# One store of the gradient of wo in two parts: 115 rows and 13 rows

## The chip, the cores and the metric

The kernel runs on one core of one Trainium2 chip. The metric is the device time of one execution in microseconds (us); of several runs the median is taken. The core has five engines with a queue of instructions each (PE for matmuls, DVE, ACT, POOL, and SP, which here only issues transfers) and 16 DMA engines, which carry all transfers between HBM and on-chip memory. SP's transfers are on queue q1 of the profile, ACT's on q10, POOL's on q0.

## The reference

The program is the forward and backward pass of a small decoder block: attention with one query token per sequence over a cache of keys and values, and a ReLU layer behind it, both with layer norm and residual.

```python
B, Sq, D = 2, 1, 640
Hq, Hkv, Sk, Dh = 32, 32, 4096, 128          # wo is (Hq * Dh, D) = (4096, 640)
q = (x @ wq).reshape(B, Sq, Hq, Dh)
p = softmax(einsum("bhqd,bhkd->bhqk", q, k) * Dh ** -0.5)
o = einsum("bhqk,bhkd->bhqd", p, v)
attn = o.reshape(B, Sq, Hq * Dh) @ wo
h  = x + attn(layernorm(x))
h2 = h + relu(layernorm(h) @ w1) @ w2
# returned: h2 and the gradients of x, k_cache, v_cache, wq, wo, w1, w2 for grad_out
```

The gradient of wo (`out_5`, 4096 x 640 in bf16) is the outer product of `o` and the gradient of `h`, summed over the two sequences. The gradients of the two caches are 64 MB each and make up nearly all that is written.

## The kernel before

The work runs in two passes over the 64 pairs of sequence and head, each pair having a key tile and a value tile of 1 MB (128 rows of 8192 B). The first pass reads both, transposes the keys on PE, forms scores and softmax, and sums the values. The second pass reads most value tiles once more, and forms one gradient tile for the values (`gV`, stored by POOL at L911) and one for the keys (`gK`, stored by POOL at L862), both made by DVE at L843. Loads are issued by SP in the order of a list written at build time (K and V tiles and the tiles of the second pass at L463, the second reading of wq at L1025).

All large tiles share a set of buffers of 1 MB. A buffer has a kind that a planner moves as the kernel goes on: "ld" for loads, "g" for `gV` and `gK`, "f" for the tiles of the weight gradients (`ot`), "q" for tiles of wq. A buffer is taken again when all of its transfer has landed, so DVE's next write into a "g" buffer waits until the last of the 16 DMA engines has finished the store from it.

The weight gradients are a background task, `fin_gen`, which is advanced by small credits between the steps of the second pass; all is settled at build time. It calls `outer_rows` for each piece of an output. For the gradient of wo there are two calls, one for each half of the 4096 rows (`s0` is 0 and 16 in heads; 2048 rows each). In a call, row `p * 16 + c` of the half belongs to partition `p` (0 to 127) and place `c` (0 to 15). The 16 places are done in groups of 6, 6 and 4, beginning at `c0` = 0, 6 and 12. For each group the function takes an "f" buffer, makes the products by matmuls of at most 512 columns (L972), copies them to bf16 on ACT (L978), and issues one store for the group on ACT's queue (L981). With six places a partition's part is 6 x 640 x 2 = 7680 contiguous bytes in HBM, so this store is 128 rows of 7680 B, 960 KB.

The six groups of this gradient are the six stores of 7680 B and 5120 B rows that are issued from 684 us to 761 us, three for each half. The store that the change touches is the second of the first half, issued at 698.21 us. Three "f" buffers go round: the next tile in the buffer of this store has its first copy at 740.76 us.

Beside it there are rows of 256 B that `store_row` (L664) puts out through SP: four stores of five rows each, for the two short outputs, two at about 798 us and two at 864.08 and 867.42 us.

Of the kernel before, what the change touches and what calls it, by code (L numbers as in the profile page):

```python
# [15 lines left out]
def kernel(  # L16
# [20 lines left out]
    nc = tc.nc  # L37

    B, Sq, D = A_x.shape
# [34 lines left out]
    def pst(shape, dtype, role, name):  # L74

        k = banks[role].pop(0)
        banks[role].append(k)
        return ps.tile(shape, dtype, tag=f"bank{k}", bufs=1, name=name)
# [11 lines left out]
    def take(tag, shape, name):  # L90
        assert free[tag] > 0, (tag, name)
        free[tag] -= 1
        k = homes[tag].pop(0)
        t = pools[k].tile(shape, BF16, tag=f"big{k}", bufs=1, name=name)
        home_of[id(t)] = (tag, k, t)
        return t
# [9 lines left out]
    def give(t, to=None, first=False):  # L106
        tag, k, _ = home_of.pop(id(t))
        to = to or goes_to(tag)
        owned[tag] -= 1
        owned[to] += 1  # L110
        free[to] += 1
        homes[to].insert(0 if first else len(homes[to]), k)
        given_at[k] = step[0]
# [8 lines left out]
    def rested(tag, n):  # L122

        return free[tag] > 0 and (forced[0] or step[0] >= given_at.get(homes[tag][0], -n) + n)
# [24 lines left out]
    def wait(n):  # L149

        end = step[0] + n * spread[0]
        while step[0] < end and not forced[0]:
            yield 0.0
        yield
# [763 lines left out]
    def rows_of(pool, col, n, name, tag):  # L918

        r = pool.tile([128, n * 128], BF16, tag=tag, bufs=2 if tag == "rD" else 1, name=name)  # L920

        def widen(c0):
            cn = min(4, n - c0)
            w = FIN["wide"][(c0 // 4) % 2]
            nc.scalar.copy(out=w[:, 0:cn, :, 0:B], in_=col[:, c0:c0 + cn, None, :].to_broadcast([128, cn, 4, B]))

        widen(0)
        yield
        yield
        for c0 in range(0, n, 4):  # L930
            cn = min(4, n - c0)
            w = FIN["wide"][(c0 // 4) % 2]
            o_busy.append(banks["o"][0])
            t = pst([128, 512], FP32, "o", "rw_ps")
            for k in range(cn):
                nc.tensor.matmul(t[:, k * 128:(k + 1) * 128], lhsT=w[:, k, :, :].rearrange("p q x -> p (q x)"),  # L936
                                 rhs=ident_bf[:], start=True, stop=True)
            nc.scalar.copy(out=r[:, c0 * 128:(c0 + cn) * 128], in_=t[:, 0:cn * 128])
            o_busy.pop(0)
            if c0 + 4 < n:  # L940
                widen(c0 + 4)
                yield 1.0
            yield 0.7
        FIN[name] = r

    FIN = {}
# [2 lines left out]
    spreading = [False]  # L949
    o_busy = []  # L950

    def outer_rows(L, r0, nrow, R, N, out_ap, cc):


        P = nrow // cc
        grp = max(1, min(cc, 4096 // N))
        out_v = out_ap.rearrange("(p c) n -> p c n", c=cc)
        for c0 in range(0, cc, grp):
            gn = min(grp, cc - c0)
            while not rested("f", 13):  # L960
                yield 0.0
            ot = take("f", [128, grp, N], "ot")
            todo = [(k, n0, min(512, N - n0)) for k in range(gn) for n0 in range(0, N, 512)]
            made = []
            for x in range(len(todo) + 1):
                if x < len(todo):
                    k, n0, nn = todo[x]
                    q = 32 * (fw[0] % 4)
                    o_busy.append(banks["o"][0])
                    o_ps = pst([128, 512], FP32, "o", "o_ps")  # L970
                    fw[0] += 1
                    nc.tensor.matmul(o_ps[0:P, 0:nn], lhsT=L[q:q + B, bass.ds(r0 + c0 + k, P, step=cc)],  # L972
                                     rhs=R[q:q + B, n0:n0 + nn], start=True, stop=True)
                    made.append((o_ps, k, n0, nn))
                    yield 0.3
                if x > 0:
                    o_ps, k, n0, nn = made[x - 1]
                    nc.scalar.copy(out=ot[0:P, k, n0:n0 + nn], in_=o_ps[0:P, 0:nn])  # L978
                    o_busy.pop(0)
                    yield 0.3  # L980
            nc.scalar.dma_start(out=out_v[:, c0:c0 + gn, :], in_=ot[0:P, 0:gn, :])  # L981
            give(ot)

    def fin_gen(fin):
        FIN["wide"] = [fin.tile([128, 4, 4, 32], BF16, tag="wide", bufs=2, name="wide") for _ in range(2)]
        for w in FIN["wide"]:
            nc.vector.memset(w[:], 0.0)
        yield from wait(2)
        yield from rows_of(fin, acol, NF, "ar", "rX")
        ar_ps = pst([128, NFF, B], FP32, "mid", "ar_ps")  # L990
        for cf in range(NFF):
            nc.tensor.matmul(ar_ps[:, cf, :], lhsT=FIN["ar"][0:B, bass.ds(cf, 128, step=NFF)], rhs=ident_bf[0:B, 0:B],
                             start=True, stop=True)
        nc.scalar.copy(out=arow[:, 0:NFF, :], in_=ar_ps[:])
        if F_rem:
            nc.scalar.copy(out=arow[:, NFF, :], in_=acol[:, NFF, :])
        yield ("arow", 0)
        yield from rows_of(fin, gc, ND, "gr", "rD")
        yield from outer_rows(FIN["ar"], 0, NFF * 128, FIN["gr"], D, out_7[0:NFF * 128, :], NFF)
        if F_rem:  # L1000
            yield from outer_rows(FIN["ar"], NFF * 128, F_rem, FIN["gr"], D, out_7[NFF * 128:Dff, :], 1)
        yield from rows_of(fin, ghfc, NF, "ghfr", "rX")
        yield from rows_of(fin, x2c, ND, "x2r", "rD")
        yield from outer_rows(FIN["x2r"], 0, D, FIN["ghfr"], Dff, out_6, ND)
        HH = H // 2
        while ("gh1", B - 1) not in done:
            yield
        yield from rows_of(fin, gh1c, ND, "gh1r", "rD")
        for s0 in range(0, H, HH):
            yield from rows_of(fin, OFc[:, s0:s0 + HH, :], HH, "OFr", "rX")  # L1010
            yield from outer_rows(FIN["OFr"], 0, HH * 128, FIN["gh1r"], D, out_5[s0 * 128:(s0 + HH) * 128, :], HH)
        yield from rows_of(fin, x1c, ND, "x1r", "rD")
        for s0 in range(0, H, HH):
            while not all(("go", B - 1, h) in done for h in range(s0, s0 + HH)):
                yield
            yield from rows_of(fin, GQc[:, s0:s0 + HH, :], HH, "GQr", "rX")
            yield from outer_rows(FIN["x1r"], 0, D, FIN["GQr"], HH * 128, out_4[:, s0 * 128:(s0 + HH) * 128], ND)
# [165 lines left out]
    for n, (i, j) in enumerate(plan):  # L1183
# [29 lines left out]
        if i is None and ("w1", 1) in done and fin is None:  # L1213
            wts.release()
            fin = tc.alloc_tile_pool(name="fin", bufs=1)
            big2 = tc.alloc_tile_pool(name="big2", bufs=1)
            more_home("f", big2)
            banks.update(sps=[2, 3], o=[4, 5, 6])
            bg2.append(("fin", fin_gen(fin)))
            bg3.append(("gx", gx_gen(fin)))  # L1220
# [23 lines left out]
        at = LIGHT if j is None else HEAVY_TAIL if open_tail else HEAVY  # L1244
# [63 lines left out]
```

## Time and profile before

| What | Value |
|---|---|
| Median of 3 runs | 892.14 us (891.62 to 892.43) |
| Profiled execution, its own time | 892.4 us |
| Its span, first to last instruction | 890.6 us |
| Busy: PE, DVE, ACT, POOL | 83%, 77%, 53%, 23% of the span |
| DMA packets, bytes, mean rate | 56304, 361.84 MB, 406 GB/s |
| Share of the DMA queues q1 (SP), q0 (POOL), q10 (ACT) | 58.1%, 36.2%, 4.1% of 16 engines |
| Last gradient tile: issue of its store | 874.91 us |

The page of the profile has the busy share of each engine over the whole span and in 40 equal slices (a digit is tenths; 9 is 90% or more), the rate of the DMA engines in the same slices, the DMA queues, the chain of work that ended last, and the costliest groups of instructions. A DMA is cut into packets, here one for each contiguous run of at most 8192 B for these tiles, and a 4 B packet closes the share of each DMA engine that takes part; the transfer is complete when all of them have closed. The trace keeps of every packet its queue, size, start and duration, but not which of the 16 engines moved it.

### The profile page before, as it was taken

What the parts mean: (1) busy time and instruction counts of PE and PEld (TensorE: products, weight loads), DVE (VectorE), ACT (ScalarE), POOL (GpSimd) and SP (SyncE); (2) the same over time, 40 slices, a digit from 0 to 9 for tenths busy, and PEclk for the clock granted to TensorE, in tenths of its full rate; (3) what the DMA queues carried; (4) which work ended last, traced back from release to release, by engine and by line L of the source; (5) the groups of instructions that cost most, each with busy time, mean ns of one, the idle gap of its engine ahead of it and who ended that gap; (6) DMA issues with size and microseconds to landing.
All of it is one profiled execution on the core that took longest, in us unless ns stands there. A gap on an engine that the chain in (4) does not pass through costs nothing. (4 is left out here: it accounts for less than half of the span.)

```text
span 890.6 us, 24645 instructions
## 1 busy us (share of the span) xinstructions
PE 740.5 (83%) x10145; PEld 622.4 (70%) x10145; DVE 687.8 (77%) x1283; ACT 469.7 (53%) x1184; POOL 204.3 (23%) x342
## 2 busy tenths in 40 slices
PE   4999899999999998888888767885888888658871
PEld 4887788888887887777777656764666665536561
DVE  2665779876789897796796888786988467899992
ACT  1344334443455665454547766554567766437751
POOL 1344434342310000000023321121323011111141
PEclk9999989999999999997995555555557765555555
DMA  9999999999889999999999999999999999999995
GB/s 377 419 411 404 409 407 419 410 415 408 350 325 369 422 422 424 422 421 424 422 390 423 420 419 420 419 416 416 391 404 413 424 425 425 424 426 424 423 421 245
DMA packets 56304, 361.84 MB, mean 406 GB/s; under 512 B 5696, under 2 KB 11904, under 8 KB 15488
## 3 DMA queue, kind: packets, MB, share of 16 engines
q1 hardware_dynamic: 34536, 211.13, 58.1%
q0 software_dynamic: 18432, 134.23, 36.2%
q10 hardware_dynamic: 3224, 14.92, 4.1%
q8 instruction: 80, 1.31, 0.6%
q14 instruction: 32, 0.26, 0.1%
HBM read 211.11 MB, written 149.13 MB: 404 GB/s over the span
## 5 line engine op out<-in xcount | busy, mean ns | idle before, releaser
L447 ACT COPY t_sb<-t_ps 128x512 f32<-128x512 f32 x479 | 273.1, 587 | 186.3 <-PE t_ps L442 181.7
L455 PEld LDWEIGHTS <-t_sb 128*128 128x128 bf16 x4096 | 169.9, 103 | 83.7 <-ACT t_sb L447 42.3
L442 PE MATMUL t_ps<-ident_f,Wt 128*128 128x128 f32 x832 | 201.0, 393 | 0.4 <-ACT t_sb L447 0.4
L483 DVE TENSOR_TENSOR pk<-Kt,ep 128x2048 bf16<-128x2048 bf16 x128 | 156.2, 1221 | 44.7 <-ACT ep L534 24.9
L476 PE MATMUL m_ps<-pk,Vt 128*128 128x129 bf16 x2048 | 176.1, 223 | 13.3 <-DMA Vt<-in_A_v_cache_dram 12.6
L843 DVE TENSOR_TENSOR gK<-rb,gsp 128x2048 bf16<-128x2048 bf16 x128 | 153.8, 1226 | 28.0 <-DMA out_dram<-gV 26.2
L843 DVE TENSOR_TENSOR gV<-rb,pp 128x2048 bf16<-128x2048 bf16 (+2 forms) x128 | 147.1, 1172 | 30.8 <-DMA out_dram<-gK 24.0
L442 PEld LDWEIGHTS t_ps<-ident_f,Wt 128*128 128x128 f32 x832 | 140.4, 205 | 31.9 <-issue 25.0
L442 PE MATMUL t_ps<-ident_f,Kt 128*128 128x128 f32 x1024 | 154.7, 287 | 4.6 <-DMA Kt<-in_A_k_cache_dram 4.5
L476 PEld LDWEIGHTS <-Vt 128*128 128x128 bf16 x2048 | 131.0, 99 | 16.9 <-DMA Vt<-in_A_v_cache_dram 14.9
L442 PEld LDWEIGHTS t_ps<-ident_f,Kt 128*128 128x128 f32 x1024 | 117.0, 148 | 6.1 <-issue 3.4
L493 POOL COPY pk<-ep 128x16 bf16<-128x16 bf16 x80 | 83.1, 1041 | 151.3 <-ACT ep L534 112.7
L455 PE MATMUL dp_ps<-gom,t_sb 128*128 128x2 bf16 x2048 | 96.0, 168 | 23.3 <-ACT t_sb L447 22.9
L911 POOL DMA_DIRECT2D out_dram<-gV x64 | 34.3, 536 | 307.8 <-DVE nb L526 114.3
L455 PE MATMUL s_ps<-gom,t_sb 128*128 128x2 bf16 x2048 | 80.2, 164 | 1.2 <-DVE t_sb L445 1.2
L862 POOL DMA_DIRECT2D out_dram<-gK x64 | 34.1, 533 | 202.0 <-DVE gK L843 156.8
L593 ACT CAST MT<-m_ps 128x128 bf16<-128x128 f32 x64 | 17.1, 266 | 116.3 <-PE m_ps L476 116.3
L978 ACT CAST ot<-o_ps 128x512 bf16<-128x512 f32 (+3 forms) x152 | 67.0, 498 | 9.7 <-DMA out_dram<-ot 8.5
L883 ACT ACTIVATE rb<-dp_ps,rt 128x256 bf16<-128x256 f32 x64 | 30.2, 472 | 46.5 <-PE dp_ps L878 44.8
L669 DVE CUSTOM_DVE_ANT_0 rows<-wo_t,rows 128x640 bf16<-128x640 bf16 x64 | 52.3, 817 | 0.4 <-ACT rows L647 0.2
L669 DVE CUSTOM_DVE_ANT_0 rows<-wqs,gqr 128x1024 bf16<-128x1024 bf16 x40 | 48.8, 1219 | 0.2
L669 DVE CUSTOM_DVE_ANT_0 rows<-w_t,rows 128x640 bf16<-128x640 bf16 (+2 forms) x58 | 45.8, 790 | 1.2 <-ACT rows L647 0.5
(194 smaller groups left out, 720.4 us busy)
## 6 DMA issues: line engine op xcount, KB each, us to landing
Kt<-in_A_k_cache_dram SPq DMA_DIRECT2D x64, 1024.0 KB, 16.4
Vt<-in_A_v_cache_dram SPq DMA_DIRECT2D x64, 1024.0 KB, 16.6
out_dram<-gV POOLq DMA_DIRECT2D x64, 1024.0 KB, 15.1
out_dram<-gK POOLq DMA_DIRECT2D x64, 1024.0 KB, 15.4
Wt<-in_A_v_cache_dram SPq DMA_DIRECT2D x52, 1024.0 KB, 11.8
out_dram<-ot ACTq DMA_DIRECT2D x6, 960.0 KB, 12.4
wq_t<-in_A_wq_dram SPq DMA_DIRECT2D x5, 1024.0 KB, 11.0
wqs<-in_A_wq_dram SPq DMA_DIRECT2D x5, 1024.0 KB, 16.1
```

The lines of the kernel that those rows point to most:

```text
L442: nc.tensor.transpose(t_ps[:, j, :], natf[:, 2 * cc:2 * cc + 2, :].rearrange("p c k -> p (c k)"), ident_f[:])
L447: nc.scalar.copy(out=t_sb[:], in_=t_ps[:])
L455: nc.tensor.matmul(dst[:, sc:sc + 2], lhsT=v[:, j, :, par], rhs=vecs[:, par, :], start=(par == 0), stop=(par == 1))
L476: nc.tensor.matmul(r["m"][:, 0:129], lhsT=r["V"][:, sc, :], rhs=r["pk"][sc // HALF][:, sc % HALF, 0:129], start=(sc == 0), stop=(sc == NSC ...
L483: nc.vector.tensor_tensor(out=p["pk"][k][:, :, 0:128].rearrange("p s (a two) -> p s a two", two=2), in0=p["K"][:, sl, :].rearrange("p s (a ...
L493: nc.gpsimd.tensor_copy(out=col, in_=e)
L669: nc.vector.tensor_tensor_reduce(out=junk[0:kc, 0:width], in0=in0, in1=in1, scale=1.0, scalar=0.0, op0=ALU.mult, op1=ALU.add, accum_out=acc)
L843: nc.vector.tensor_tensor(out=pairs_view(dst[:, sl, :]), in0=row.rearrange("p (a two) -> p a two", two=2)[:, None, :, :].to_broadcast([128 ...
L862: nc.gpsimd.dma_start(out=natural(out_2, bp, hp), in_=gK[:])
L883: nc.scalar.activation(out=rb[:], in_=bank[:, 128:384], func=ACT.Copy, scale=rt[:, b, h:h + 1])
L911: nc.gpsimd.dma_start(out=natural(out_3, b, h), in_=gV[:])
L978: nc.scalar.copy(out=ot[0:P, k, n0:n0 + nn], in_=o_ps[0:P, 0:nn])
```

## The change

The store of group `c0` = 6 in the first half goes out as two DMAs one behind the other on ACT's queue: partitions 0 to 114, then partitions 115 to 127. The buffer is given back after both. All other calls have an empty table and issue one store as before.

```diff
+    CUTS = {6: (0, 115, 128)}
+
-    def outer_rows(L, r0, nrow, R, N, out_ap, cc):
+    def outer_rows(L, r0, nrow, R, N, out_ap, cc, cuts=()):
...
-            nc.scalar.dma_start(out=out_v[:, c0:c0 + gn, :], in_=ot[0:P, 0:gn, :])
+            at = dict(cuts).get(c0, (0, P))
+            for p0, p1 in zip(at, at[1:]):
+                nc.scalar.dma_start(out=out_v[p0:p1, c0:c0 + gn, :], in_=ot[p0:p1, 0:gn, :])
             give(ot)
...
-            yield from outer_rows(FIN["OFr"], 0, HH * 128, FIN["gh1r"], D, out_5[s0 * 128:(s0 + HH) * 128, :], HH)
+            yield from outer_rows(FIN["OFr"], 0, HH * 128, FIN["gh1r"], D, out_5[s0 * 128:(s0 + HH) * 128, :], HH,
+                                  CUTS if s0 == 0 else ())
```

## The prediction, made before the changed kernel was run

> **What bounds the kernel now.** I read the page first, its slices and its queues, then the same stretches finer for the end, then the chain that ended last, then the packet records.
>
> ```profile
> PE   4999899999999998888888767885888888658871
> ...
> DVE  2665779876789897796796888786988467899992
> ...
> DMA  9999999999889999999999999999999999999995
> GB/s 377 419 411 404 409 407 419 410 415 408 350 325 369 422 422 424 422 421 424 422 390 423 420 419 420 419 416 416 391 404 413 424 425 425 424 426 424 423 421 245
> ...
> q10 hardware_dynamic: 3224, 14.92, 4.1%
> ```
>
> No compute engine is full in every slice, DMA is, but for the last. From slice 32 (690 us) on the rate stands at 421 to 426 GB/s: the transfers set the time. 425 GB/s over 16 engines is 26.6 GB/s for one. How the end comes about is in the stretches (times, then five engines' busy time, clock, DMA share, GB/s):
>
> ```profile
> 874.00:880.00 6.00, 0.00 (x0) 0.00 (x0) 0.61 (x1) 0.00 (x0) 0.53 (x1) 0.50 1.02 423
> 880.00:882.00 2.00, 0.00 (x0) 0.00 (x0) 0.00 (x0) 0.00 (x0) 0.00 (x0) 0.50 0.53 221
> 882.00:888.60 6.60, 0.00 (x0) 0.00 (x0) 0.00 (x0) 0.00 (x0) 0.00 (x0) 0.50 0.06 27
> ```
>
> Until 880 us all 16 engines work; from 882 to 888.5 us the share is 0.06, which is 1/16, and the rate 27 GB/s, that of one engine. **One DMA engine is late by itself, and it alone sets the end.** The completions of the last gradient store say it again: the median of its sixteen is at 881.5 us, the fifteenth at 882.95, the sixteenth at 888.92. The two chain lines to read are these:
>
> ```profile
> 803.34 31.36 DMA out_dram<-gV
> ...
> 874.89 0.56 POOLq L1303
> ```
>
> A store issued at 803.34 us lands 31 us later, so stores queue up far ahead of the late engine; the last one is issued at 874.91 us and lands 14 us later. From 698 us on every gradient store lands 13.6 us or more after its issue, its sixteenth completion 6 to 16 us behind the median one: I find no moment after 698 us at which the late engine is without work. So whatever is added to this engine after 698 us moves the end one for one, and what is added to others is free up to their slack, 882.95 against 888.92, or 6.0 us.
>
> **Which engines a store uses.** The packets of q10 can be counted: 2900 data packets (768 of 7680 B, 1280 of 4096, 256 of 6912, 256 of 5120, 192 of 1280, 128 of 3456, 20 of 256) leave 324 closing ones, which is 19 stores by 16 plus two loads of ten rows by 10. The five-row stores of SP near the end:
>
> ```profile
> q1 hardware_dynamic: 20, 0.00, 0.1%
> ...
> out_dram<-rows SPq DMA_DIRECT2D x2, 1.2 KB
> ```
>
> Twenty packets for two stores: five of data and five closing ones each. So 128 and 64 rows use 16 engines, 10 use 10, 5 use 5, and in every one of these all engines get equally many rows (8, 4, 1, 1). 115 is 5 x 23, so equal shares of 115 rows exist for 5 engines with 23 rows, or for one; 13 rows give 13 engines one row each. The other end is uneven sharing: 8 rows on fourteen engines and 3 on a fifteenth. I take five, because no transfer of this trace has uneven shares. The Trainium skill (DMA: Bandwidth & Descriptors, "Why a DMA increments its semaphore by 16 and not by 1") gives the number of engines as the largest one up to 16 that divides the slowest dimension, and takes the lowest-numbered ones. By it 23 rows go to engines 0 to 4, one each to 0 to 12, and the sum is the one below; the trace agrees in 16, 10 and 5, and has no engine numbers.
>
> **Is the late engine one of the five?** A five-row store marks its five engines with 256 B packets. On a busy engine a packet starts 3 or 4 ns before the recorded end of the one before, so a chain can be followed back from the last packet (888.486 us), with eight 8 KB packets and one closing packet for each store. It closes stores at 876.23, 873.77, 871.24, 868.63 and 865.97 us, all links exact, and holds the 256 B packets at 871.213 and 867.604 us with their closing ones: one of each five-row store, as an engine of the five must. The sixteenth completions of those stores come 0.48 to 0.51 us after this chain's closing packets; the nearest chain without row packets would have them 0.50, 0.44 and then 0.26 us after. I take the late engine as one of the five, not as certain.
>
> **The change part by part.**
> - Late engine, removed: 8 rows of 7680 B. Added: 23 rows and 1 row. That is 16 rows more. The 128 packets of the store at 698.21 us take 291.5 ns each, 288 ns with the overlap, so **+16 x 0.288 = 4.6 us**. With uneven shares it would be 9 rows for 8, +0.3 us; with the late engine outside the five, 0 or 1 rows for 8, -2.3 or -2.0 us. All of it lies on the path that sets the end.
> - The other four of the five: also +4.6 us, in their slack of 6.0 us, so nothing. The remaining eleven lose 7 or 8 rows, which frees time that nobody waits for.
> - One closing packet more on five engines (9 ns): nothing.
> - One issue more on ACT, 0.34 us. It stands in front of work on ACT only if ACT has any:
>
> ```profile
> 698.21 0.34 ACTq L981 DMA_DIRECT2D out_dram<-ot  x1
> 699.80 1.01 ACT L1043 COPY gqr<-gq_ps 128x1024 bf16<-128x1024 bf16 x1 [1.08 <-PE gq_ps L653]
> ```
>
> The next copy starts at 699.80 us after 1.08 us of waiting for PE, which covers it; uncovered it would be 0.35 us on an engine that is 53% busy.
> - The `ot` buffer comes back later. Now the store lands at 710.09 us. 15 more packets on one engine, each with one or two packets of q0 and q1 between, are 15 x 0.6 to 0.9 = 9 to 14 us, so 719 to 724 us; the next copy into the buffer is at 740.76 us. Nothing; if that cover were gone, ACT would stop with PE's copies behind it.
> - "g" buffers come back up to 4.6 us later, as the late engine's stores do, and DVE's waits (to 785 and 835 us) end later by as much. It is the same 4.6 us, not a second time: at 874.91 us the late engine still has 14 us of stores ahead.
>
> Sum against the profiled execution: span 890.6 + 4.6 = 895.2, and 1.8 us around it, 897.0 from 892.4. The median of the runs is 0.3 us below that execution, so 892.14 + 4.6 = **896.7 us**, +0.5%. What a measurement of this kernel can tell from no change is about 0.2%, 1.8 us.
>
> **The rivals.**
> - *Relief instead of load (faster).* The late engine is not one of the five. Then it loses 7 or 8 rows, and its end goes from 888.9 to 886.6 or 886.9. The five end by 882.95 + 4.6 = 887.5 at the latest, so the gain is 1.4 to 2.3 us: 890.1 with 2.0. It decides from the identity of one engine. For it: the lateness is in q0, and none of q0's packets says where. Against it: the chain with the two row packets. The Trainium skill (same page, "Latency and other measured facts") says that DMA engines 7 and 15 are usually the slow ones, with stores of POOL suspected; those lie outside the first five, and by that rule the time would be this rival's. The trace speaks against it, through the same two packets.
> - *No effect.* The rows are shared out unevenly (+0.3 us), or the late engine runs dry once and the added rows sink into that gap: 892.1 to 892.4. Against it: equal shares everywhere, and a queue that is never short. The change then wouldn't do what its uneven numbers suggest. The skill's advice not to split a transfer by partitions, as the parts serialise on the same engines (same page, "Rules for kernel authors"), would also give this.
> - *More than the rows (slower).* Loads on five engines come late as well, and DVE or PE wait for a tile that they now have in time, or ACT stops at the buffer: one more stop of 3 to 5 us that the late engine's queue does not cover, 900 to 902. Against it: 14 us of backlog and 17 to 30 us of room at the buffer.
>
> **How the numbers follow.** Forecast case 0.74 (896.7; its own range 895 to 898.5, as the packets vary from 291 to 300 ns and the stores ahead may pile up differently); more than the rows 0.06; no effect 0.10; relief 0.10, of which 0.08 beyond 0.2% and 0.02 within. Slower 0.80, same 0.12, faster 0.08. The range takes in the no-effect case below and some of a stop above: 892.0 to 899.0, with relief and a full stop left out.
>
> **What would show each step.** In the packets of the changed kernel q10 has 3226 instead of 3224 (18 x 16 + 5 + 13 + 20 closing ones): right for the 5 and 13 engines; 3236 would mean 15 and 13. The stretch with a DMA share of 1/16 at the end should be about 4.6 us longer on the profile of before, 10 to 11 us, or the single engine be joined by four at a share up to 0.3 for some us. The chain should still end in a store's landing, and ACT's idle time before L978 not grow. I am wrong if the span shrinks with a shorter tail (relief), or if the tail stays 6.6 us with the 5 and 13 engines seen (another engine is the late one, or there was a gap to sink into).

## The result and the profile after

| Kernel | Median, us | Ratio to before, 95% interval | Profiled execution and its span, us |
|---|---|---|---|
| before (6 runs beside it) | 892.28 (890.84 to 894.08) | 1 | 892.4, 890.6 |
| changed (6 runs) | 898.50 (897.42 to 900.28) | 1.0070 [1.0055, 1.0086] | 897.42, 895.6 |

The change costs 6.2 us in this series (4.9 to 7.7 by the interval), where 4.6 was forecast. In a second series, shown below, the same kernel cost 4.6 us (2.9 to 6.4). The profiled execution is 5.0 us longer.

From the page of the changed kernel: the slices of DMA share and rate, and the queue of ACT.

```profile
DMA  9999999999989999999999999999999999999995
GB/s 379 418 412 403 409 406 420 410 413 410 361 332 370 422 423 424 422 422 423 416 389 423 418 418 417 418 420 420 393 410 411 394 408 424 420 423 418 423 386 234
...
q10 hardware_dynamic: 3226, 14.92, 4.1%
```

The 3226 packets on q10 are those of shares on 5 and on 13 engines. Slices 32 and 33 (694 to 739 us, the cut store is issued in the first) are new: 394 and 408 GB/s where the kernel before has 424 and 425, with the DMA share at 9 as before. Slice 39 (851 to 873 us) is lower too, 386 for 421; it comes up again at the end. Finer, the stretch of 20 us behind the cut store, of before and then of after (time, then the five engines' busy time, clock, DMA share, GB/s):

```profile
700.00:720.00 20.00, 16.32 (x208) 13.71 (x207) 7.47 (x8) 15.11 (x27) 2.62 (x6) 0.76 1.02 426
```

```profile
700.00:720.00 20.00, 17.26 (x187) 14.63 (x188) 7.13 (x7) 13.95 (x25) 1.31 (x3) 0.59 1.01 381
```

The last two columns are to be read together. The engines are as fully busy as before (1.01 and 1.02) and move 11% less. So they aren't idle: single packets take longer. The queues of the same 20 us (packets, MB, share of 16 engines), before and after:

```profile
q0 software_dynamic: 518, 3.76, 44.8%
q1 hardware_dynamic: 510, 3.75, 44.5%
q10 hardware_dynamic: 144, 0.98, 11.7%
```

```profile
q0 software_dynamic: 500, 3.62, 49.7%
q1 hardware_dynamic: 426, 3.08, 36.5%
q10 hardware_dynamic: 124, 0.89, 14.5%
```

POOL's stores (q0) and the cut store (q10) hold more engine time for fewer bytes, and SP's loads (q1) get what is left. In the packet records of these 20 us the 7680 B packets of the cut store take 400 ns on the mean, up to 2167 ns, where they took 291 ns; the 8 KB packets of the gradient stores take 359 ns for 311. The loads' packets keep their 309 ns.

The end of the changed kernel, in the same columns:

```profile
882.00:884.00 2.00, 0.00 (x0) 0.00 (x0) 0.00 (x0) 0.00 (x0) 0.00 (x0) 0.50 1.02 422
884.00:886.00 2.00, 0.00 (x0) 0.00 (x0) 0.00 (x0) 0.00 (x0) 0.00 (x0) 0.50 0.62 258
886.00:888.00 2.00, 0.00 (x0) 0.00 (x0) 0.00 (x0) 0.00 (x0) 0.00 (x0) 0.50 0.15 61
888.00:890.00 2.00, 0.00 (x0) 0.00 (x0) 0.00 (x0) 0.00 (x0) 0.00 (x0) 0.50 0.10 41
890.00:892.00 2.00, 0.00 (x0) 0.00 (x0) 0.00 (x0) 0.00 (x0) 0.00 (x0) 0.50 0.07 29
892.00:894.00 2.00, 0.00 (x0) 0.00 (x0) 0.00 (x0) 0.00 (x0) 0.00 (x0) 0.50 0.04 16
```

Three shares can be told apart: until 884 us all 16 engines work; from 886 to 890 us the share falls from 0.15 to 0.10, two engines or a few; and only from 890 us on it is that of one engine. The last gradient store is issued at 879.89 us, 5.0 us later than before. Its sixteen completions have their median at 885.54 us, the fifteenth at 889.82, the sixteenth at 893.87. Before, they were at 881.5, 882.95 and 888.92. So the late engine ends 8.3 us behind the median, where it was 7.4. **Nearly all of the 5 us lies ahead of the tail**: the pipeline comes 4 to 5 us later to the last store, and the tail itself grows by about 1 us. The chain that ended last has the same links as before, each later by 5 us:

```profile
808.31 31.36 DMA out_dram<-gV
...
879.87 0.55 POOLq L1308
```

Slice 39 has another reason than slices 32 and 33. The stretch ahead of the end, of before and then of after:

```profile
850.00:874.00 24.00, 17.46 (x174) 15.02 (x174) 23.62 (x40) 12.23 (x28) 11.29 (x16) 0.50 1.01 418
```

```profile
850.00:874.00 24.00, 19.06 (x184) 16.55 (x185) 23.66 (x41) 12.11 (x26) 9.71 (x15) 0.50 0.94 388
```

Here the share itself falls, to 0.94: some DMA engines have nothing to do at times. That fits a late engine for which the others wait. Of the kernels that cut one store, those with 115 and 13 rows show it (0.94, 0.97 and 0.90 in three executions), and the three others of the experiments below have 1.01 here; but with the marks of experiment 4 the kernel before is at 0.97 too.

The issue of the two parts on ACT's timeline (start, duration, what, and the idle time ahead of it with its releaser):

```profile
697.35 1.54 ACTq L985 DMA_DIRECT2D out_dram<-ot  x2
698.95 1.01 ACT L1048 COPY gqr<-gq_ps 128x1024 bf16<-128x1024 bf16 x1 [1.09 <-PE gq_ps L653]
```

The second issue takes 1.2 us, not 0.34. The copy behind it still waits for PE and not for the issue.

### The profile page after: what moved, and what is told of

The parts are those of the page before. It is cut to its first block, busy times and chain, and to the rows that moved or that the text cites. A ratio compares the mean times of both kernels' runs of the same rounds, so it can differ in the third digit from the quotient of the medians.

```text
span 895.6 us, 24647 instructions
## 1 busy us (share of the span) xinstructions
PE 738.4 (82%) x10145; PEld 619.0 (69%) x10145; DVE 687.2 (77%) x1283; ACT 468.8 (52%) x1184; POOL 204.7 (23%) x342
## 3 DMA queue, kind: packets, MB, share of 16 engines
q10 hardware_dynamic: 3226, 14.92, 4.1%
## 5 line engine op out<-in xcount | busy, mean ns | idle before, releaser
L442 PE MATMUL t_ps<-ident_f,Kt 128*128 128x128 f32 x1024 | 149.8, 281 | 4.8 <-DMA Kt<-in_A_k_cache_dram 4.3
L442 PEld LDWEIGHTS t_ps<-ident_f,Kt 128*128 128x128 f32 x1024 | 113.2, 145 | 6.5 <-PE m_ps L476 3.8
```

Source lines behind the costliest of these rows:

```text
L442: nc.tensor.transpose(t_ps[:, j, :], natf[:, 2 * cc:2 * cc + 2, :].rearrange("p c k -> p (c k)"), ident_f[:])
```

## The experiments

Four questions were open: whether it is the issue or the uneven rows that costs, which engine is late, whether a wait behind the store adds to it, and what the longer packets hang on. Theory A is the forecast's (16 rows more on the late engine, one of the first five).

**1. The cut alone, with even shares.** The same store in two parts, 112 and 16 rows, so that every engine keeps its 8 rows:

```diff
-    CUTS = {6: (0, 115, 128)}
+    CUTS = {6: (0, 112, 128)}
```

> The store goes out in two parts of 112 and 16 rows: as many DMAs and issues as in the change, but 7 + 1 = 8 rows for each of 16 engines, as before. Theory A (16 rows more on the late engine, one of the first five): no change against the kernel before, ratio 0.998 to 1.002. Theory B (the second issue on ScalarE's queue and its wait, 1.54 us in place of 0.34 us, is what costs): as slow as the changed kernel, ratio 1.005 to 1.009. Theory C (any engine loaded with 24 rows holds up loads, buffers and stores, whichever engine is late): no change, as A.

Measured: 893.26 us, ratio 1.0005 [0.9996, 1.0015], q10 with 3240 packets (16 and 16 closing ones). Two parts by themselves cost nothing that the timed runs can measure. Theory B is out: the two issues took 2.37 us here, longer than the 1.54 us of the changed kernel. The Trainium skill (DMA: Bandwidth & Descriptors, "Rules for kernel authors") advises against splitting a transfer over partitions, since the halves serialise on the same engines; the trace agrees in so far as nothing is gained.

**2. Sixteen rows on the first engine, and on the first three.** Cuts at 17 and 32, and at 51 and 64. In the first, engine one gets 24 rows and the fifth 7; in the second the first three get 22 rows and the fifth 5.

```diff
-    CUTS = {6: (0, 115, 128)}
+    CUTS = {6: (0, 17, 32, 128)}
```

and in the other kernel:

```diff
-    CUTS = {6: (0, 115, 128)}
+    CUTS = {6: (0, 51, 64, 128)}
```

> Three parts of 17, 15 and 96 rows: if a DMA uses the largest number of engines up to 16 that divides its rows, beginning with the first, then the first engine gets 17 + 1 + 6 = 24 rows, the fourteen after it 7, the last 6. Theory A: 897 us or some 5 to 6 us over the kernel before (ratio 1.005 to 1.008) if the first engine is the late one; otherwise its 4.6 us lie in its slack of 6 us and the late engine loses one row: no change, ratio 0.997 to 1.002. Theory B: slower by the issues, 1.005 or more. Theory C: slower, 1.004 to 1.009, whichever engine is late.

> Three parts of 51, 13 and 64 rows: 17 + 1 + 4 = 22 rows for the first three engines, 5 for the next ten, 4 for the last three. Theory A: slower by 14 rows, 4 us or a little more (ratio 1.004 to 1.007), if the late engine is among the first three; if it is the fourth or fifth, it loses 3 rows, 0.9 us, and the time is at or just under the kernel before (0.996 to 1.001). Theory B: 1.005 or more. Theory C: 1.004 to 1.009 in either case.

Measured: 894.38 us, ratio 1.0026 [1.0013, 1.0040], and 895.07 us, ratio 1.0035 [1.0023, 1.0047]; q10 has 3240 packets in both (1 + 15 + 16 and 3 + 13 + 16 closing ones). Both cost, +2.3 and +3.1 us, although the engine that was to be the only one that matters is, as experiment 4 shows, relieved by one and by three rows. There is a cost that isn't the late engine's own rows. No theory had these numbers: they lie above the ranges of A (up to 1.002 and 1.001 with this engine late) and below those of C (from 1.004).

**3. The cut in both halves.** The table is given to both calls, so that two stores put 16 rows more on the first five.

```diff
-                                  CUTS if s0 == 0 else ())
+                                  CUTS)
```

> The same cut of 115 and 13 rows in both halves of the gradient, so two stores of this form: 32 rows more on each of the first five engines. Theory A: twice the loss, 2 x 4.6 = 9.2 us by the rows, 12 us if what the changed kernel measured (6.2 us) doubles: ratio 1.010 to 1.014. Theory B: about twice too. Theory C (a loss once, when five engines fall behind the others and the others run short): less than twice, 1.007 to 1.010.

Measured: 903.85 us, ratio 1.0127 [1.0114, 1.0140], +11.3 us, which is 1.8 times the first series' 6.2 and 2.5 times the second's 4.6. A second cut costs about as much as the first, as theories A and B had it, and not less, as C had.

**4. Which engine is late?** The last five-row store of 256 B rows is moved to the very end and cut into pieces whose packets have a size for each number of engines: 40 B in the piece of five rows, 44 in that of four, 48, 52 and 72 B in those of three, two and one. An engine's chain of packets, followed back from its last, then tells its place: all five sizes on the first engine, only 40 on the fifth.

```diff
+    MARKS = ((0, 5, 0, 20), (0, 4, 20, 42), (0, 3, 42, 66), (0, 2, 66, 92), (0, 1, 92, 128),
+             (4, 5, 20, 128), (3, 4, 42, 128), (2, 3, 66, 128), (1, 2, 92, 128))
...
-        nc.sync.dma_start(out=dst, in_=r[0:n])
+        for r0, r1, n0, n1 in marks or ((0, n, 0, 128),):
+            nc.sync.dma_start(out=dst[r0:r1, n0:n1], in_=r[r0:r1, n0:n1])
...
+            while b == B - 1 and not forced[0]:
+                yield 0.0
```

It was put into the kernel before, the changed kernel and both kernels of experiment 2.

> The kernel before, with the last five-row store moved behind the last gradient tile and cut by columns into pieces of 5, 4, 3, 2 and 1 rows and four more single rows, each piece with a row size of its own (40, 44, 48, 52 and 72 B; the single rows 72, 124, 172 and 216 B). If a DMA of n rows takes the first n engines, the fifth engine gets a 40 B packet alone, the fourth 40 and 44, the third 40, 44, 48, the second those and 52, the first all. The chain of the last closing packet then names the late engine. Theory A (late engine one of the first five, the same in each execution): the last chain holds the 40 B packet and tells which of the five; time 892 to 894 us. Theory D (the late engine is another one): no mark in the last chain.

> The changed kernel with the same marks. Theory A: the last chain holds the same marks as in the kernel before with marks, and the next ones to end belong to others of the first five; time 897 to 900 us. Theory D: one of the five loaded engines has taken the place of another late engine, so the marks of the last chain differ from those of the kernel before.

> The store of 17, 15 and 96 rows with the same marks. It measured 0.26% over the kernel before, half of what 16 rows on the late engine cost. Theory A as worked out: the late engine is not the first; its chain ends last, and the first engine (all nine marks) ends up to 4.6 us later than in the kernel before with marks, but under it. Theory D2 (the late place changes hands): the first engine ends last, and the loss is its 4.6 us less the 2 to 3 us by which it was ahead.

> The store of 51, 13 and 64 rows with the same marks; it measured 0.35% over the kernel before. Theory A with the late engine among the second and third: it ends last, 4 us after that of the kernel before with marks. With the fourth or fifth late, it would end 0.9 us earlier than before; Theory D2: one of the first three ends last in its place, after 4.0 us less its lead.

Measured, one profiled execution each (the kernel before without marks took 893.10 us beside them):

| With marks | Time, us | Ends last, and its marks | Others |
|---|---|---|---|
| before | 891.50 | 887.580, only 40: the fifth | 886.167, no mark; the first at 881.3 |
| changed | 897.96 | 894.028, only 40: the fifth | |
| 17, 15 and 96 rows | 894.11 | 890.155, only 40: the fifth | the first at 889.005 |
| 51, 13 and 64 rows | 894.76 | 890.799, all five sizes: the first | the fifth at 890.071, the second at 889.911 |

The late engine is the fifth, in the kernel before and in the changed one; with 51, 13 and 64 rows the first, with its 14 rows more, has overtaken it by 0.7 us. The rule of the Trainium skill on engines 7 and 15 (DMA: Bandwidth & Descriptors, "Latency and other measured facts") stood in the forecast as a rival; these chains decide for the fifth. The next latest engine of the kernel before has no mark at all, so it lies outside the first five. Relieved by one and by three rows the fifth doesn't end earlier than in the kernel before but 2.6 and 2.5 us later; with 16 more rows, 6.4 us later.

Most of the 2.5 us isn't the cut's. These executions stood apart before it: the packets had moved 276 MB, a point ahead of the first of the six stores, at 676.7 us in the kernel before with marks, and at 679.2, 678.1 and 679.0 us in the three others (changed, 17 rows, 51 rows). Counted from there, the fifth ends 1.2 and 0.3 us later than before where it is relieved, and 4.0 us later with 16 more rows. So the 17 and 19 rows between the cases are worth 2.8 and 3.7 us, where 0.288 us a row would make 4.9 and 5.5. With one execution each these are rough sizes.

**5. The wait on SP, and a control.** In the changed kernel one load of SP waits for the 115-row store (SP's queue: who waits, for what, us in total, times, longest):

```profile
SPq L463 <- DMA out_dram<-ot: 3.1, 1, 3.1
```

The load has nothing to do with that store. By the semaphore events of the trace the completion semaphores go round among the DMAs, and the load's turn falls on the one that the 115-row part still holds; it lands at 723.3 us, and the load is issued at 723.37 us, where it had been issued at 719.68 us before. Issued in the other order the long part holds a semaphore whose next user comes later.

```diff
-            for p0, p1 in zip(at, at[1:]):
+            for p0, p1 in reversed(list(zip(at, at[1:]))):
```

> The changed kernel with the two parts issued in the other order, 13 rows first and 115 rows after: the same rows on the same DMA engines, but the late 115-row part now carries the other completion semaphore, whose next user on SP's queue is a load issued about 18 us later, so that no load of SP need wait for the landing of the 115 rows. Theory A (the 16 extra rows on the late engine, and what the overloaded engines do to the loads behind them, are the whole cost): the same as the changed kernel, ratio to before 1.006 to 1.008, and in the waits of SP's queue the 3.1 us on the store is gone without a gain. Theory E (the load that waited 3.1 us for the store's landing makes the 1 to 1.6 us above the 4.6 us of the rows): ratio about 1.005, 896.9 to 897.3 us where before is 892.3.

> The changed kernel unchanged, beside the two others of this series on the same chip, as their control. Both theories: ratio to before 1.0055 to 1.0085.

Measured in one series: swapped 897.42 us, ratio 1.0042 [1.0027, 1.0056]; unchanged again 897.56 us, ratio 1.0052 [1.0033, 1.0072]. The wait is 4.4 us in the control's trace and absent from the swapped one's, and the medians differ by 0.1 us. The wait is real, and these runs show no cost of it; a cost of 1 us, which theory E gave it, lies within their intervals and isn't excluded. Alone, 1.0042 would have looked like theory E's 1.005; the control fell below its range as well. It shows how far a series can be trusted: the same kernel gave 1.0070 and 1.0052. Over these three measurements (the changed kernel twice, the swapped one once) the mean is 1.0055, 4.9 us.

**6. The same idea in small doses.** All six stores of this gradient in five parts, 112 rows and four times 4: each gives the first four engines 3 rows more and the fifth one fewer. If rows are what matters, the end should come 1.7 us earlier.

```diff
-    CUTS = {6: (0, 115, 128)}
+    CUTS = {c: (0, 112, 116, 120, 124, 128) for c in (0, 6, 12)}
...
-                                  CUTS if s0 == 0 else ())
+                                  CUTS)
```

> Six stores of the gradient of wo (three in each half) go out as 112 rows and four parts of 4 rows: each gives the first four DMA engines 3 rows more than in the kernel before and every other engine, the late fifth among them, 1 row fewer. Over the kernel the fifth carries 6 rows fewer, 1.7 us at 0.288 us a row, and the first four 18 more, 5.2 us, spread over six stores. Theory A with the rows of the late engine alone: 1.7 us faster, ratio 0.998. Theory E' (an engine loaded ahead of the others delays the loads behind it, which costs even where the late engine is relieved): ratio 1.000 to 1.004, as the stores that gave the first one or three engines 16 rows at once cost 1.0026 and 1.0035; spread by 3 rows (0.9 us) at a time the delay should mostly be absorbed, so 0.999 to 1.001 if a delay under a microsecond is free.

Measured: 906.06 us, ratio 1.0146 [1.0126, 1.0166], +13 us. Every expectation was far off. The trace shows a thing that no kernel had shown so far, on ACT's timeline:

```profile
769.85 12.62 ACTq L985 DMA_DIRECT2D out_dram<-ot  x5
782.57 1.24 ACT L980 CAST ot<-o_ps 128x512 bf16<-128x512 f32 x3 [12.21 <-DMA out_dram<-ot]
```

Five issues hold ACT's queue for 12.6 us, and the copies behind them wait for as long.

**7. Is it the rows or the number of DMAs?** The same 30 DMAs, with even shares:

```diff
-    CUTS = {c: (0, 112, 116, 120, 124, 128) for c in (0, 6, 12)}
+    CUTS = {c: (0, 64, 80, 96, 112, 128) for c in (0, 6, 12)}
```

> The same six stores in five parts each as in the run before (which gave ratio 1.0146, its extra DMAs on ScalarE's queue holding ScalarE for 2 to 12.6 us a store), but cut at 64, 80, 96 and 112 rows, so that every part has a multiple of 16 rows and every DMA engine gets the same bytes as in the kernel before. Theory U (it was the rows put on four engines that cost): ratio 0.999 to 1.002, each store's five issues in 2 to 4 us. Theory N (it was the 24 more DMAs, with their issues on ScalarE's queue and their completion semaphores, that cost): ratio 1.008 to 1.015, with issues of 5 to 12 us again.

Measured: 907.01 us, ratio 1.0155 [1.0131, 1.0180], with issues of 3 to 10 us a store. With even shares it costs as much: **it is the number of DMAs**, 24 more for 13.8 us, 0.58 us each. In what way isn't settled: the issues hold ACT for 39 us in the six stores, and packets take longer, and no run has one without the other. One more would be 0.6 us, 0.06%, and the first experiment (0.05%, up to 0.15%) can't see that. The stretch of 760 to 800 us in the kernel before, and then in this one:

```profile
760.00:800.00 40.00, 21.89 (x192) 16.35 (x190) 35.77 (x52) 15.80 (x36) 5.88 (x12) 0.54 1.01 426
```

```profile
760.00:780.00 20.00, 11.48 (x108) 7.93 (x107) 11.35 (x18) 7.84 (x19) 1.39 (x4) 0.50 0.97 353
780.00:800.00 20.00, 8.62 (x82) 6.04 (x81) 11.80 (x17) 6.68 (x16) 2.40 (x5) 0.50 1.00 360
```

Again the share of the DMA engines is full or nearly so, at 353 and 360 GB/s where the kernel before had 426. DVE is busy for 23 us of 40 where it had been for 36.

**All together: how much longer the packets take.** From the packet records: of every packet of 8192, 7680, 5120 or 1280 B that starts between 690 and 840 us, what it takes above the usual time of its size in the kernel before (309, 291, 196 and 55 ns), summed and divided by 16 engines. The cost by timed runs is the ratio's excess times 892.3 us. But executions stand up to 3.4 us apart when they have moved 276 MB, before anything differs. So the last column has, for the execution that the packets are from, the time from 276 MB moved to the last packet, over the 209.9 us of the kernel before.

| Kernel | More DMAs | Longer packets, us | Same, over before | Cost, timed runs, us | Later from 276 MB on, us |
|---|---|---|---|---|---|
| before | 0 | 0.5 | | | |
| 112 + 16 | 1 | 1.7 | 1.1 | 0.4 | 1.6 |
| 17 + 15 + 96 | 2 | 2.5 | 1.9 | 2.3 | 0.7 |
| 51 + 13 + 64 | 2 | 4.5 | 4.0 | 3.1 | 1.4 |
| 115 + 13, first series | 1 | 3.8 | 3.3 | 6.2 | 6.2 |
| 115 + 13, again | 1 | 3.7 | 3.1 | 4.6 | 3.7 |
| 13 + 115 | 1 | 4.4 | 3.9 | 3.7 | 6.5 |
| 115 + 13, both halves | 2 | 7.0 | 6.4 | 11.3 | 11.7 |
| 112 and 4 times 4, six stores | 24 | 11.4 | 10.9 | 13.0 | 11.2 |
| 64 and 4 times 16, six stores | 24 | 13.1 | 12.5 | 13.8 | 13.1 |

The three kernels that cut one store and leave the fifth engine alone come 0.7 to 1.6 us later; with the marks, counted from the marked kernel before, 17 and 51 rows give 1.2 and 1.3. The four executions with 115 and 13 rows in one store, the marked one with 4.0 among them, come 3.7 to 6.5 us later. The means are 1.2 and 5.1 us. So there are two costs: a cut into uneven parts costs something whichever engine gets the rows (of even parts only the one trace says so), and the rows on the late engine cost some 3.9 us on top by the traces, or about 2 us by the timed runs (4.9 less 2.3 to 3.1).

How much longer the packets take is not the price by itself. The stretch of 20 us behind the cut with 112 and 16 rows, and then with 51, 13 and 64:

```profile
700.00:720.00 20.00, 17.74 (x183) 14.48 (x182) 7.81 (x9) 13.98 (x25) 2.61 (x6) 0.50 1.01 403
```

```profile
700.00:720.00 20.00, 17.80 (x153) 14.36 (x153) 9.45 (x9) 12.68 (x22) 1.84 (x4) 0.50 1.01 377
```

Both show a full share at a lower rate, the second one a lower rate than the changed kernel's 381 GB/s, and both cost less than the changed kernel. That longer packets of engines that end before the late one sink, in part, into their slack would explain it; it isn't shown. Where 24 DMAs are added, cost and lengthening are of one size (11 to 14 us), in both ways of counting.

## Why the prediction was right, point by point

- *DMA is full in every slice but the last.* Two slices (11 and 12) read 8, with 350 and 325 GB/s; from slice 32 on, which the argument needs, it holds.
- *The late engine sets the end, and it is one of the five.* Shown: it is the fifth in the kernel before and in the changed one. The chain with the two row packets pointed the right way, but isn't the only one: with links of 2 to 5 ns there are several ways back from the last packet, and some hold no row packet. It took the marks to settle it.
- *115 rows on 5 engines, 13 on 13.* Shown by the 3226 packets, and the same rule by the closing packets of all other cuts (17 on 1, 51 on 3, 15 on 15, 4 on 4).
- *16 rows at 0.288 us, one for one, 4.6 us.* The total came out near that: 6.2, 4.6 and, in the other order, 3.7 us; 898.50 us lies at the upper end of the range. The mechanism is shown, as a cut costs less when the 16 rows go to other engines. Its size came out in part by luck: the rows measured about 2 us by the timed runs and 2.8 to 3.9 us by the traces, so less than forecast, and a term put at nothing made up for it. Which of the two is nearer wasn't settled. The 0.288 us is the time of a packet when no store is cut; right behind the cut the packets take 0.400 us.
- *The other four of the five, and the loads on them: nothing, in their slack of 6.0 us.* This is the mis-sized term. Uneven parts of which the fifth has no share cost 2.3 and 3.1 us by the timed runs, and 0.7 to 1.4 us by the traces. The slack was read at the end, on the last store; the packets take longer between 695 and 725 us, where all 16 engines are full. At most part of it sank into the slack.
- *The eleven that lose rows have free time that nobody waits for.* Right behind the cut there was none: at a share of 1.01 the stretch moved 381 GB/s for 426. It came 150 us later, as a share of 0.94 from 850 to 874 us, and nothing was gained by it.
- *One more issue on ACT, 0.34 us, hidden by 1.08 us.* It took 1.2 us, and was hidden all the same, by 1.09 us. At one cut this made no difference; at five parts a store it holds ACT for up to 12.6 us.
- *The `ot` buffer is back at 719 to 724 us.* It was, at 723.3 us, and the next copy into it didn't wait. The idle time ahead of all `ot` copies went from 9.7 to 8.3 us.
- *The "g" buffers come back 4.6 us later, the same 4.6.* Right in kind: the last store is issued 5.0 us later and lands 5.0 us later, not 10. DVE's waits for stores of gradient tiles, from 690 us on, grew from 28.2 to 37.5 us, while 3.8 us of waits for ACT fell away.
- *The stretch with one engine at the end would be 4.6 us longer, or joined by four.* Neither quite: the tail grew by 1 us and the pipeline moved by 5, which is what the previous point says and the sign overlooked. The fifteenth completion was 4.1 us ahead of the sixteenth, for 6.0 before.
- *The rivals.* Relief: out, the late engine is the fifth. No effect: out, all intervals lie above 1. More than the rows: there is a cost beside the rows, with loads that get 36.5% of the engines' time behind the cut for 44.5%, but of DVE and PE neither has a new wait for a load. SP's stop of 3.1 to 4.4 us at the store's semaphore had no cost that these runs could tell.

## What to carry to other kernels

When all DMA engines are full, cost a cut of a transfer by what it does to all transfers beside it, not only by the rows of the engine that ends last: read the DMA share and the rate in one line, as a full share at a lower rate means packets that take longer. That is a sign and not the price: here the price depended more on whether the engine that ends last gets more to do. To tell the two apart, give the same rows to other engines, as experiment 2 does. Cut by multiples of 16 rows if at all, and count DMAs: one more cost nothing measurable here, 24 more cost 13.8 us though bytes and shares stayed the same. Slack read at the end of a kernel doesn't safely cover a cost that arises in the middle of it. And before traces of two executions are compared, look how far apart they stood before anything differed: here up to 3.4 us, as much as what was to be explained.

## What the runs showed of the hardware that was not expected

- Cutting a store on one queue makes the packets of stores on another queue take longer: in 700 to 720 us those of POOL's gradient stores went from 311 to 359 ns, single ones to 1.6 us, while loads kept their 309 ns. With even parts (112 and 16) it was 323 ns. In the kernel with 24 more DMAs 8 KB packets of loads take longer too (363 ns in 760 to 800 us). Why, no run shows.
- A DMA issue can hold its engine for microseconds: 0.34 us is what one took before, 1.2 us for the second part of the cut store (2.0 us with 112 and 16 rows), and up to 12.6 us for five. What it waits for isn't in the profile; it was seen only where several DMAs followed each other on one queue while the DMA engines were full.
- In the kernel before the last completion came 6.0 us after the fifteenth, and with the marks the fifth engine ended 1.4 us after the next and 6.3 us after the first. All it has to do beyond engines outside the five (rows of 256 B, shares of the ten-row loads) the first engine has as well. Why the fifth is late stays open.
- The Trainium skill (DMA: Bandwidth & Descriptors, "Why a DMA increments its semaphore by 16 and not by 1") says that the number of engines is the largest divisor up to 16 and that the lowest-numbered ones are taken. The traces agree with the divisors in every cut tried, and the marks agree with nested sets: the engine of a one-row piece is in all the larger ones.
